# Attention with a soft mixture of experts: which side of the products with v is stationary

## The chip, the cores and the metric

The kernel runs on one core of a Trainium2 chip. The metric is the device time in microseconds (us) of one execution. A core has a matrix engine (TensorE, PE in the profile, its loads of the stationary side PEld), a vector engine (DVE), a scalar engine (ACT), GpSimd (POOL) and a queue engine (SP) that issues the DMAs. A product takes a stationary side, loaded first, and streams a moving side past it; the result's partitions are the stationary side's columns.

## The reference

```python
def _attn_ref(q, k, v, s):                       # 8 batches, 8 heads, 576 rows, 64 columns
    scores = scale * np.matmul(q, k.transpose(0, 1, 3, 2))
    cum = np.cumsum(np.maximum(s, 0.0), axis=-1)
    bias = -(cum[:, :, :, None] - cum[:, :, None, :])
    scores = np.where(causal, -1000000000.0, scores + np.minimum(bias, 0.0))
    attn = np.exp(scores - np.max(scores, axis=-1, keepdims=True))
    attn = attn / (np.sum(attn, axis=-1, keepdims=True) + 1e-09)
    return np.matmul(attn, v)

def _moe_ref(x, phi, w1, w2):                    # x: 4608 x 512, the heads beside each other
    logits = x @ phi                             # 32 slots, 4 for each of 8 experts
    d = softmax of logits over the rows; c = softmax of logits over the slots
    slot_out[e] = relu((d.T @ x)[e] @ w1[e]) @ w2[e]
    return c @ slot_out
```

(The two softmax lines are shortened to words.) q and k come eight times larger than drawn. All inputs are float32.

## The kernel before, in words

Two heads make a pair: 32 pairs, four to a batch. A pair's head 0 lies on partitions 0 to 63 and head 1 on 64 to 127. The 576 rows are cut into chunks: as keys j = 0 to 4 (four of 128, one of 64).

`scores(p)` (L254 to L434) makes a pair's exponentials. q and k are loaded (`load`, L265), copied in a shorter float32 form (`cast`, L278, ACT) and the rest kept beside it (`low`, L283, DVE). The row maxima come from a first product of q and k (`mx`, L311, PE) reduced on DVE (`red`, L323); `f0`, `f1`, `f2`, `md` (L335 to L361) split the maxima in a high and a low part, turn them, and write them by DMA as extra rows of a small tile `gt`, which also holds two rows of the cumulated s. The scores proper (`s`, L377, 48 products a pair) sum three products of q and k parts and a fourth with `gt`, which adds the bias and subtracts the maximum. ACT takes the exponential out of PSUM (`ex`, L388) and POOL zeroes the masked triangle (`cut`, L395). The exponentials lie in the arena as keys on partitions and queries along the row. POOL then sums them over the key chunks (`z`, L421 to L427), ACT copying the first chunk (L414).

`pair(p)` (L440) makes the output of the attention. v is stationary with its 64 columns of a head, the exponentials of key chunk j move, up to 512 queries at a time: `a` (L478) into y, and `ax` (L467) for the first 64 queries into x. The result has the head's columns on partitions and queries along the row. ACT copies it (L486, L490). `sm` (L507) sums z over the keys with a stationary side that holds one column of ones, for the four pairs of a batch into one bank. Per batch `e1` (L595, L596) adds 1e-9 and takes reciprocals, `rw` (L600) writes them to DRAM, and `rd` (L517) reads them back broadcast to 64 partitions each. `nr` (L540, DVE) scales the result in u; for the last pair `rb` (L528) spreads the reciprocals by products. `nat` (L548) transposes u back to rows on partitions, and `natd` (L555, ACT) copies it into x of the batch.

`batch(b)` (L589) makes logits from u (`lt`, L619, L623), and the softmaxes and the sums over rows (`c0` to `t8`); `t7` (L771) multiplies by x. After all pairs, sit (L941) and the experts' two layers (L954, L988) and the output (L1020 and the copies after it) follow. The experts' weights are 64 tiles of 512 KB: NPRE = 21 are fetched during attention into `pre`; the others go where attention's buffers become free (`room`), the last ones where first-layer weights have been used.

The order of every engine is fixed before the run by `schedule` (L34): each step has an engine, an estimated time, a priority (a table `PR` of offsets on top of 2 x pair), what it must follow, and how many of the six PSUM banks it takes. The y and sum banks are kept apart. `busy` (L914) puts filler products on PE where the plan leaves it idle before the first product with v and after the last.

Of the kernel before, what the change touches and what calls it, by code (L numbers as in the profile page):

```python
# [17 lines left out]
NEG = -3.0e38  # L18
NG = 3

PR = dict(load=-9.063, load_v=-9.132, cast=(9.576, 4.001), cum=-25.895, low=(4.9, 44.265), mx=(-6.08, 10.156, 8.807,
          8.159), red=(2.144, 3.397, 3.057, -37.226), f0=-0.714, f1=30.964, f2=0.529, md=-6.393, s=(-65.95, -10.099,
          -16.585, -0.002), ex=(6.942, -14.568, 1.896, 3.855), cut=(1.377, -17.534, 2.864, 12.095), zc=3.583,
          z=(1.07, -54.955, 7.483, 3.74), ax=102.687, a=(136.656, 0.022, -2.121, 0.386, -0.338), evx=-22.47,
          ev=-3.276, sm=14.037, e1=-1.61, rw=24.679, rd=-39.652, nstep=4.53, nr=1.749, nat=48.432, natd=-28.53,
          lt=-51.395, nat0=116.745, natd0=17.779, c0=4.561, c1=-16.819, soft=15.188, tok=30.263, LA=161.4, ct=1.864,
          T2=-19.79, LP=176.8, gap=0.81401)
NBUF = (2, 2, 2, 1, 5, 2, 3)
NBANK = 6
GAP = 300  # L30
NPRE = 21
# [71 lines left out]
def tile_attn_softmoe(ctx: ExitStack, tc, qk, v, s, phi, w1, w2, cst, out):  # L103
# [37 lines left out]
    NR, NPB, NV, NZ, NU, NQ, NW = NBUF  # L141
    PAD = 64
    size = dict(raw=2 * S, p=3200, u=S, v=640, z=2 * S, r=S, x=NCH * DM)
    place = [(kind, (NP + i) % n) for kind, n in (("raw", NR), ("p", NPB), ("z", NZ), ("v", NV), ("r", NQ), ("u", NU), ("x", 1))
# [10 lines left out]
    def slot(kind, shape, dtype, name):  # L155
        return keep.tile(shape, dtype, tag=kind, name=name, bufs=dict(g=NG, w=NW)[kind])
# [16 lines left out]
    s_sb = reg("x", 0)[0:NH, 0:S]  # L173
    ones_s = reg("x", 0)[0:NH, S:2 * S]
    cum = reg("x", 0)[0:NH, 2 * S:3 * S]
    nc.sync.dma_start(out=s_sb, in_=s)
    nc.vector.memset(ones_s, 1.0)
    nc.vector.tensor_scalar(s_sb, s_sb, 0.0, 8.0, op0=ALU.max, op1=ALU.mult)
    nc.vector.tensor_tensor_scan(out=cum, data0=ones_s, data1=s_sb, initial=0.0,
                                 op0=ALU.mult, op1=ALU.add)  # L180
    cumhl = reg("x", 0)[0:NH, 0:2 * S].rearrange("p (l x) -> p l x", l=2)
    nc.vector.tensor_copy(cumhl[:, 0, :].bitcast(F32R), cum)
    nc.vector.tensor_tensor(cumhl[:, 1, :].bitcast(F32R), cum, cumhl[:, 0, :], op=ALU.subtract)
    cumd = pd.tile([NH, 2, S], F32, tag="cum", name="cumd", bufs=1)


    SQ = S // 8
    onesl = one.tile([128, 4 * HP, 32], F32, name="onesl")
    nc.vector.memset(onesl, 0.0)
    for a in range(4 * HP):  # L190
        nc.vector.memset(onesl[:, a, a:a + 1], 1.0)

    dn = one.tile([128, 2, 128], F32, name="dn")
    nc.vector.memset(dn[64:128, 1, :], 0.0)
    nc.gpsimd.memset(reg("x", 0)[64:128, 0:DM], 0.0)
    for i in range(NV):
        nc.gpsimd.memset(reg("v", i)[64:128, 512:640], 0.0)
    for i in range(NPB):
        nc.gpsimd.memset(reg("p", i).rearrange("p (a x) -> p a x", a=2)[64:128, :, 1536:1600], 0.0)
    ph = one.tile([128, HP, 4 * NS], F32, name="ph")  # L200
# [4 lines left out]
    gs = []  # L205
    for i in range(NG):
        t = slot("g", [128, PAD + 2 * S], F32R, f"g{i}")
        if i == 1:

            mask = one.tile([128, S], F32, name="mask")  # L210
            nc.gpsimd.memset(mask, 0.0)
            nc.gpsimd.affine_select(mask[:, S - 128:S], mask[:, S - 128:S], pattern=[[-1, 128]], compare_op=ALU.is_ge,
                                    fill=NEG, base=0, channel_multiplier=1)
        (nc.vector if i else nc.gpsimd).memset(t.bitcast(F32), 0.0)
        for a in (0, 64):
            nc.gpsimd.memset(t[a:a + 4, 0:KO].bitcast(F32), 1.0)
            nc.gpsimd.memset(t[a:a + 4, KO:].bitcast(F32), -1.0)  # L217
        gs.append(t)
# [5 lines left out]
    ones2 = one.tile([128, 128], F32R, name="ones2")  # L224
    nc.vector.memset(ones2.bitcast(F32), 0.0)
    for a in (0, 64):
        nc.vector.memset(ones2[a:a + 2].bitcast(F32), 1.0)  # L227
    mx = []
    for i in range(3):
        t = one.tile([128, 2, NCH], F32, name=f"mx{i}")  # L230
        nc.vector.memset(t, 0.0)
        mx.append(t)

# [20 lines left out]
    def scores(p):  # L254

        t0 = 2.0 * p
        gt, w = gs[p % NG], ws[p % NW]
# [13 lines left out]
        op(("load", p), "SP", 400, (t0, "load"), load,  # L271
# [8 lines left out]
        def low(i):  # L280
            use("raw", p, NR)
            use("w", p, NW)
            nc.vector.tensor_tensor(w[:, QO + S * (2 + i):QO + S * (3 + i)], st["raw", p][:, i, :],  # L283
                                    w[:, QO + S * i:QO + S * (i + 1)].bitcast(F32), op=ALU.subtract)
        g = old(NW)
        war = [("s", g, i) for i in range(4)] if g is not None else []
        for i in range(2):
            op(("cast", p, i), "ACT", 565, (t0, ("cast", i)), (cast, i), [("load", p)] + war)
            op(("low", p, i), "DVE", 950, (t0, ("low", i)), (low, i), [("cast", p, i)])
# [90 lines left out]
        def ex(i, a):  # L380
            if ("p", p) not in st:
                own("p", p, NPB)
                st["p", p] = reg("p", p % NPB).rearrange("p (a x) -> p a x", a=2)
# [729 lines left out]
```

## Time and profile before

| | us |
|---|---|
| median of 3 runs (440.46 to 441.74) | 441.44 |
| the profiled execution | 441.82 |
| its span, first to last instruction | 440.1 |
| PE busy | 406.3 |
| PE's loads (PEld) busy | 302.5 |
| DVE busy | 309.6 |
| POOL busy | 281.4 |
| ACT busy | 245.4 |

The mean granted clock of TensorE is 0.978. A group of instructions is shown as: line, engine, operation, what is written from what (partitions of the moving side * columns of the stationary side for PE), shape, count | busy time in us, mean time of one in ns | idle time before and what ended it. The time of one product includes its way through the array, so neighbours overlap; their pace is the distance of their starts. In the chain of waits a line is start, length and what ran, in us, and in the timeline start, length from the first start to the last end, and the instructions merged.

### The profile page before, as it was taken

Reading aid. Unit: us, or ns where it says so; the run is one execution under the profiler, and the core shown is the slowest. Engines: PE = TensorE matmul, PEld = TensorE weight load, DVE = VectorE, ACT = ScalarE, POOL = GpSimd, SP = SyncE. Lnnn points to the kernel's source line nnn. Section 1 sums busy time; section 2 is a strip of 40 time slices with the busy share of each in tenths; the row PEclk is TensorE's granted clock in tenths of the full one; section 3 lists DMA queues with packets and bytes.
Section 4 is the critical chain, followed back from the end, with each engine's and each line's share of the span. In section 5 each row is a group of like instructions: output and inputs, shape, how many; then the busy total and the mean of one; then the engine's idle time right before and its main releaser. Section 6 shows DMA issues by size and latency. Waiting matters only on the chain.

```text
span 440.1 us, 14686 instructions
## 1 busy us (share of the span) xinstructions
PE 406.3 (92%) x5625; PEld 302.5 (69%) x5625; DVE 309.6 (70%) x1055; ACT 245.4 (56%) x732; POOL 281.4 (64%) x385
## 2 busy tenths in 40 slices
PE   7999999989999999999999999999999999898960
PEld 6787777777677767766877687777776857344550
DVE  6777767987887888779877887788778486121460
ACT  3146676576658665856675676567665745011350
POOL 7349889878877895888588858887887710000000
PEclk9599999999999999999999999999999999999995
DMA  5317565626664475448544822362247389999988
GB/s 175 108 57 236 157 174 155 212 87 189 193 180 131 137 217 157 131 136 225 152 132 136 231 90 84 105 178 82 87 114 216 95 291 337 392 402 409 384 297 293
DMA packets 54549, 83.21 MB, mean 189 GB/s; under 512 B 5456, under 2 KB 41808, under 8 KB 54480
## 3 DMA queue, kind: packets, MB, share of 16 engines
q1 hardware_dynamic: 54480, 82.29, 59.6%
q8 instruction: 44, 0.72, 0.7%
q14 instruction: 25, 0.20, 0.1%
HBM read 71.84 MB, written 10.06 MB: 186 GB/s over the span
## 4 chain that ended last, share of the span: by engine, by line
PE 66%; DMA 12%; DVE 9%; issue 5%; SPq 3%; POOL 2%; ACT 1%; DVEq 0%
PE s L377 19%; PE y L478 15%; PE mx L311 10%; DMA arena<-rs 7%; PE m L954 3%; DMA rs<-sr 3%; PE m L988 3%; PE sum L507 3%; SPq L517 2%; DVE nmin L733 2%; PE busy L914 2%; PE lt L619 2%; PE nat L548 2%; PE po L1020 2%; DVE junk L323 1%
## 5 line engine op out<-in xcount | busy, mean ns | idle before, releaser
L323 DVE CUSTOM_DVE_ANT_0 junk<-mx,mask 128x448 bf16<-128x448 f32 (+3 forms) x320 | 125.5, 427 | 50.8 <-PE mx L311 25.1
L388 ACT ACTIVATE arena<-s 128x288 f32<-128x288 f32 (+4 forms) x384 | 114.3, 409 | 30.0 <-PE s L377 29.3
L377 PE MATMUL s<-w 64*128 64x288 f32 (+4 forms) x1152 | 109.2, 304 | 0.0
L478 PE MATMUL y<-arena 128*64 128x512 f32 (+4 forms) x640 | 90.1, 427 | 0.0
L377 PEld LDWEIGHTS s<-w 64*128 64x128 f32 (+1 forms) x1152 | 81.7, 177 | 10.1 <-ACT arena L388 1.2
L395 POOL TENSOR_SCALAR_AFFINE_SELECT arena<-arena 128x256 f32<-128x256 f32 (+1 forms) x160 | 69.0, 444 | 23.7 <-ACT arena L388 21.7
L478 PEld LDWEIGHTS y<-arena 128*64 128x64 f32 x640 | 43.0, 137 | 46.4 <-issue 35.8
L421 POOL TENSOR_TENSOR arena<-arena 128x896 f32<-128x896 f32 x31 | 66.4, 2141 | 7.5 <-PE mt L346 5.2
L311 PE MATMUL mx<-w 64*128 64x288 f32 (+4 forms) x384 | 59.3, 314 | 3.7 <-DVE e_nat L664 2.7
L311 PE MATMUL mx<-g,ones 64*128 64x288 f32 (+4 forms) x384 | 56.0, 308 | 1.7 <-DVE ones L227 1.7
L377 PE MATMUL s<-g 64*128 64x288 f32 (+4 forms) x384 | 56.5, 291 | 0.0
L423 POOL TENSOR_TENSOR arena<-arena 128x640 f32<-128x640 f32 x31 | 48.0, 1547 | 2.6
L278 ACT CAST w<-arena 128x576 fp32r<-128x576 f32 x64 | 39.8, 675 | 15.0 <-DMA arena<-in_qk_dram 15.0
L283 DVE TENSOR_TENSOR w<-arena,w 128x576 fp32r<-128x576 f32 x64 | 48.0, 776 | 0.0
L311 PEld LDWEIGHTS mx<-w 64*128 64x128 f32 x384 | 41.1, 190 | 8.1 <-PE s L377 3.8
L490 ACT COPY arena<-y 128x512 f32<-128x512 f32 x32 | 18.8, 588 | 47.0 <-PE y L478 47.0
L311 PEld LDWEIGHTS mx<-g,ones 64*128 64x128 f32 x384 | 41.0, 191 | 2.4 <-POOL g L217 1.9
L540 DVE TENSOR_TENSOR arena<-arena 128x576 f32<-128x576 f32 x31 | 34.7, 1128 | 8.7 <-DMA arena<-rs 8.4
L377 PEld LDWEIGHTS s<-g 64*128 64x128 f32 (+1 forms) x384 | 35.1, 177 | 0.7 <-DMA g<-hl 0.2
L338 POOL TENSOR_SCALAR mh<-mx 128x10 fp32r<-128x10 f32 x32 | 21.5, 672 | 20.4 <-DVE mx L323 20.3
L425 POOL TENSOR_TENSOR arena<-arena 128x384 f32<-128x384 f32 x31 | 31.4, 1013 | 2.4
L323 DVE CUSTOM_DVE_ANT_0 junk<-mx,mask,mx 128x288 bf16<-128x288 f32 x64 | 30.6, 516 | 2.2 <-PE mx L311 1.2
(157 smaller groups left out, 565.8 us busy)
## 6 DMA issues: line engine op xcount, KB each, us to landing
pre<-in_w_dram SPq DMA_DIRECT2D x38, 512.0 KB
arena<-in_qk_dram SPq DMA_DIRECT2D x32, 576.0 KB
arena<-in_w_dram SPq DMA_DIRECT2D x18, 512.0 KB
arena<-rs SPq DMA_DIRECT2D x62, 144.0 KB
arena<-in_v_dram SPq DMA_DIRECT2D x32, 256.0 KB
out_dram<-arena SPq DMA_DIRECT2D x11, 512.0 KB
out_dram<-pre SPq DMA_DIRECT2D x7, 512.0 KB
wg<-in_w_dram SPq DMA_DIRECT2D x5, 512.0 KB
```

The source lines that it names most:

```text
L278: nc.scalar.copy(w[:, QO + S * i:QO + S * (i + 1)], st["raw", p][:, i, :])
L283: nc.vector.tensor_tensor(w[:, QO + S * (2 + i):QO + S * (3 + i)], st["raw", p][:, i, :], w[:, QO + S * i:QO + S * (i + 1)].bitcast(F32), ...
L311: nc.tensor.matmul(ps[a][:, d:d + hi - lo], l[r], t[r, KO + lo:KO + hi], start=t is w, stop=t is gt)
L323: nc.vector.tensor_tensor_reduce(out=junk[r, 0:w], in0=ps[r, d:d + w], in1=mask[r, o:o + w], scale=1.0, scalar=m[:, a, 4:5] if i == 1 else ...
L377: nc.tensor.matmul(ps[a][0:n, d:d + hi - lo], t[r, ko + 128 * j:ko + 128 * j + n], t[r, qo + lo:qo + hi], start=x == 0, stop=x == 3)
L388: nc.scalar.activation(st["p", p][0:n, a, o + lo:o + hi], ps[0:n, d:d + hi - lo], AF.Exp, bias=0.0, scale=0.125)
L395: nc.gpsimd.affine_select(d, d, pattern=[[0, 2], [1, n]], compare_op=ALU.is_ge, fill=0.0, base=0, channel_multiplier=-1)
L421: eng.tensor_tensor(z[:, :, 128:576], pt[:, :, 128:576], pt[:, :, 576:1024], op=ALU.add)
L423: eng.tensor_tensor(z[:, :, 256:576], z[:, :, 256:576], pt[:, :, 1024:1344], op=ALU.add)
L425: eng.tensor_tensor(z[:, :, 384:576], z[:, :, 384:576], pt[:, :, 1344:1536], op=ALU.add)
L478: nc.tensor.matmul(y[r, lo - 64:512], vt[:, j, r], st["p", p][:, g, OFF[j] + lo - 128 * j:OFF[j] + 576 - 128 * j], start=(j == 0), stop=(j ...
L540: nc.vector.tensor_tensor(u, u, st.pop(("r", p)), op=ALU.mult)
```

## The change

The exponentials become the stationary side, 128 queries at a time, and v moves: the 64 columns of a head and a 65th column of ones beside them. The result has queries on partitions, in two banks: y0 for the query chunks 0 to 2 and y1 for 3 and 4, both heads side by side. Query chunk c needs the key chunks 0 to c. The 65th column is the row sum, so `z`, `sm`, `e1`, `rw`, `rd`, `rb` and `nr` go, with their buffers; `norm` on DVE adds 1e-9, takes the reciprocal and multiplies out of PSUM. `nat` now turns rows on partitions into columns on partitions for `lt`, which follows it. The query chunks are 0 to 3 of 128 rows and 4 of 64.

`gt`, the ones beside it, the mask and the split maxima become bfloat16; the cumulated s takes three rows instead of two. One of a pair's two `low` steps goes from DVE to POOL. v comes in three DMAs instead of two. NPRE goes from 21 to 26, with smaller buffers in the arena and the `gt` tiles no longer used for weights. Pair 0 gets precedence over all else in the plan, the setup is reordered, and the plan's priorities are another set.

```diff
-NBUF = (2, 2, 2, 1, 5, 2, 3)
+NBUF = (2, 2, 2, 5, 6, 3)
-NPRE = 21
+NPRE = 26
...
-    size = dict(raw=2 * S, p=3200, u=S, v=640, z=2 * S, r=S, x=NCH * DM)
+    size = dict(raw=2 * S, p=3264, u=512, v=650, x=NCH * 128)
...
+    cumhl = scr[:, 0:3 * S // 2].bitcast(BF16).rearrange("p (l x) -> p l x", l=3)
+    for l in range(3):
+        nc.vector.tensor_copy(cumhl[:, l, :], cum)
+        if l < 2:
+            nc.vector.tensor_tensor(cum, cum, cumhl[:, l, :], op=ALU.subtract)
...
-        t = slot("g", [128, PAD + 2 * S], F32R, f"g{i}")
+    gs = [one.tile([128, PAD + 2 * S], BF16, name=f"g{i}") for i in range(NG)]
...
+        nc.gpsimd.memset(x[:, :, :, 64:65], 1.0)
...
+        tu = t0 - 200 * (p == 0)
...
-            nc.vector.tensor_tensor(w[:, QO + S * (2 + i):QO + S * (3 + i)], st["raw", p][:, i, :],
+            (nc.vector if i else nc.gpsimd).tensor_tensor(w[:, QO + S * (2 + i):QO + S * (3 + i)], st["raw", p][:, i, :],
                                     w[:, QO + S * i:QO + S * (i + 1)].bitcast(F32), op=ALU.subtract)
...
-            nc.tensor.transpose(ps[0:4 * NCH, 0:128], mh.rearrange("p a l c -> p (a l c)").bitcast(F32), ident)
+            st["mt", p] = ps[0:4 * NCH, 0:64].bitcast(BF16)
+            nc.tensor.transpose(st["mt", p], mh.rearrange("p a l c -> p (a l c)"), identb)
...
+    yb = [psy.tile([128, 512], F32, tag=f"y{i}", name=f"y{i}") for i in range(2)]
...
+            for g in range(2):
+                c = 128 * hp + 64 * g
+                nc.sync.dma_start(out=vt[:, 0:4, g, 0:64],
+                                  in_=v[b * S:b * S + 512, c:c + 64].rearrange("(j p) c -> p j c", p=128))
+            nc.sync.dma_start(out=vt[0:64, 4, :, 0:64],
+                              in_=v[b * S + 512:b * S + 576, 128 * hp:128 * hp + 128].rearrange("p (g c) -> p g c", g=2))
...
-            for g in range(2):
-                r = slice(64 * g, 64 * g + 64)
-                nc.tensor.matmul(y[r, lo - 64:512], vt[:, j, r],
-                                 st["p", p][:, g, OFF[j] + lo - 128 * j:OFF[j] + 576 - 128 * j],
-                                 start=(j == 0), stop=(j == 4))
+        def av(c):
+            vt = st["v", p]
+            x = reg("p", p % NPB)
+            for g in range(2):
+                y = yb[c // 3][:, 130 * (c % 3) + 65 * g:130 * (c % 3) + 65 * g + 65]
+                for j in range(c + 1):
+                    o = 1600 * g + OFF[j] + 128 * (c - j)
+                    nc.tensor.matmul(y, x[:, o:o + 128], vt[:, j, g, :], start=(j == 0), stop=(j == c))
+
+        def norm(i):
+            n = 3 - i
+            y = yb[i][:, 0:130 * n].rearrange("p (c g d) -> p c g d", c=n, g=2)
+            r = p2.tile([128, n, 2, 1], F32, tag=f"rc{i}", name=f"rc{i}_{p}")
+            nc.vector.tensor_scalar(r, y[:, :, :, 64:65], 1e-9, None, op0=ALU.add)
+            nc.vector.reciprocal(r, r)
+            nc.vector.tensor_tensor(st["x", p][:, 3 * i:3 * i + n, :].rearrange("p c (g d) -> p c g d", g=2), y[:, :, :, 0:64],
+                                    r.broadcast_to([128, n, 2, 64]), op=ALU.mult)
...
-        at_ = (860, 752, 540, 325, 112)
+        for c in range(5):
+            op(("a", p, c), "PE", 236 * (c + 1), (t0, ("a", c)), (av, c), need[c] + ([("a", p, c - 1)] if c else []))
+        for i in range(2):
+            op(("n", p, i), "DVE", (680, 540)[i], (t0, ("n", i)), (norm, i),
+               [("a", p, 2 + 2 * i)] + war + ([("cw",)] if 2 <= p < NX else []))
+        op(("nat", p), "PE", 434, (t0, "nat"), nat, [("n", p, 0), ("n", p, 1)], bank=1)
...
+                st["u0", b] = p2.tile([128, HP, 64], F32, tag="u0", name=f"u0{b}", bufs=1)
...
-                nc.tensor.matmul(ps[32 * g:32 * g + 32, :], dn[:, 0, 32 * g:32 * g + 32], xn[:, g + 1, :],
-                                 start=True, stop=False)
+                r = slice(128 * hp, 128 * hp + 128)
+                for g in range(4):
+                    nc.tensor.matmul(ps[32 * g:32 * g + 32, r], dn[:, 0, 32 * g:32 * g + 32], xn[:, g, :],
+                                     start=hp == 0, stop=False, skip_group_check=True)
```

More of the change, by code (lines that the diff above doesn't have):

```diff
@@ L155, in slot @@
     def slot(kind, shape, dtype, name):
-        return keep.tile(shape, dtype, tag=kind, name=name, bufs=dict(g=NG, w=NW)[kind])
+        return keep.tile(shape, dtype, tag=kind, name=name, bufs=NW)
     def reg(kind, i):
@@ L180, in tile_attn_softmoe @@
                                  op0=ALU.mult, op1=ALU.add)
[L181 to L191, printed above, removed]
@@ L287, in scores @@
         for i in range(2):
[L288 to L289 removed]
+            op(("cast", p, i), "ACT", 565, (tu, ("cast", i)), (cast, i), [("load", p)] + war)
+            op(("low", p, i), "DVE" if i else "POOL", 950 if i else 1400, (t0, ("low", i)), (low, i), [("cast", p, i)])
         def cum():
             for a in range(2):
[L293 removed]
+                nc.sync.dma_start(out=gt[64 * a:64 * a + 3, KO:KO + S],
                                   in_=(cumhl if p < HP else cumd)[2 * p + a:2 * p + a + 1, :, :])
@@ L483, in evx, with nat, natd @@
+        def nat():
+            use("x", p, NX)
+            x = st["x", p]
+            ps = bank(f"nat{p}")
+            st["nat", p] = ps
+            for c in range(4):
+                nc.tensor.transpose(ps[:, 128 * c:128 * c + 128], x[:, c, :], ident)
+        def natd():
             own("u", p, NU)
@@ L589, in batch, with dep_n @@
+        wu = [("lt", p - NU)] if p >= NU else []
+        op(("natd", p), "ACT", 480, (t0, "natd"), natd, [("nat", p)] + wu, frees=[(("nat", p), 0)])
+    def dep_n(p, i):
+        return ("n", p, i) if p >= 0 else None
     def batch(b):
@@ L836, in fetch @@
         nc.sync.dma_start(out=dst, in_=src)
-    for e, ns in (("DVE", 5200), ("POOL", 4200), ("SP", 1100), ("ACT", 2900), ("PE", 1100)):
+    for e, ns in (("DVE", 7000), ("POOL", 6200), ("SP", 700), ("ACT", 2900), ("PE", 1100)):
         op(("set", e), e, ns, (-1000,), lambda: None)
+    for i in range(1, NG):
+        op(("gi", i), "POOL", 2400, (2.0 * i - 10,), (ginit, i), [("set", "POOL")])
     for p in range(NP):
@@ L911, in busy @@
     def busy(n):
-        d = psy.tile([128, 512], F32, tag="y", name="busy")
+        d = yb[0]
         for i in range(n):
@@ L919, in tile_attn_softmoe @@
         if ops[key]["eng"] == "PE":
-            early = early and key[0] not in ("ax", "a")
+            early = early and key[0] != "a"
             n = int((t - end - 200) / GAP)
```

347 lines of the change are left out of this document (100 added, 247 removed).

## The prediction

> **What bounds the kernel now.** I read the page first, then the engines' busy time by stretch, then the products of one source line alone, to count head pairs.
>
> ```profile
> span 440.1 us, 14686 instructions
> ...
> PE 406.3 (92%) x5625; PEld 302.5 (69%) x5625; DVE 309.6 (70%) x1055; ACT 245.4 (56%) x732; POOL 281.4 (64%) x385
> ```
> ```profile
> 11.00:22.00 11.00, 10.04 (x53) 8.22 (x54) 7.92 (x40) 1.44 (x3) 3.82 (x11) 0.53 0.36 108
> 60.00:300.00 240.00, 231.85 (x3464) 177.88 (x3464) 195.18 (x675) 157.11 (x480) 196.46 (x256) 1.00 0.54 155
> 345.00:378.00 33.00, 30.56 (x407) 22.00 (x405) 22.06 (x60) 17.60 (x59) 8.12 (x11) 1.00 0.80 274
> 378.00:420.00 42.00, 39.15 (x442) 19.07 (x442) 10.05 (x17) 7.96 (x15) 0.00 (x0) 1.00 1.03 393
> ```
> ```profile
> 60.00:300.00 240.00, 85.73 (x1096) 71.61 (x1096) 1.00 0.54 155
> ```
>
> The columns of a stretch are its length, then PE, PEld, DVE, ACT and POOL busy time, the granted clock, the DMA share and GB/s. Between 60 and 300 us, the steady part of attention, PE is busy 231.85 of 240 us at clock 1.00; the next engine, POOL, has 196 and DMA 0.54. The last fence is the same stretch for L377 alone: a pair has 48 score products, so 1096 of them are 22.8 pairs, 10.5 us each. PE sets the pace: what the change adds to PE per pair counts 32 times, and what it takes from POOL, DVE, ACT or the queues counts only where PE waits, which is 8.15 us in those 240.
>
> **The products with v, taken out.** The timeline gives the block of L478 from its start to the next block's start; the chain of waits gives L467 and L507.
>
> ```profile
> 207.11 0.66 PE L548 MATMUL nat<-ident,arena 128*128 128x128 f32 x4 [1.05 <-DVE mx L323]
> 207.70 2.81 PE L478 MATMUL y<-arena 128*64 128x512 f32 x20
> 210.44 0.67 PE L377 MATMUL s<-w 64*128 64x288 f32 x6
> ```
> ```profile
> 308.55 0.23 PE x L467 x8
> ...
> 192.55 0.64 PE sum L507 x32
> ```
>
> Ten products of v are 20 instructions, two passes for each float32 product, and take 210.44 − 207.70 = 2.74 us. The x products of two pairs are 0.23, so 0.12 a pair; the row sums are 0.64. Out go 2.74 + 0.12 + 0.64 = 3.50 us of PE per pair.
>
> **The products put in.** Per pair there are 15 blocks (c, j), two heads each, two passes each: 60 instructions. Each now moves only 65 columns, but has 128 columns of exponentials as its own stationary side, where v had 64. What one costs depends on which is longer, the load or the moving side. The trace has no product of just this form, so I bound it from both sides.
>
> ```profile
> L478 PEld LDWEIGHTS y<-arena 128*64 128x64 f32 x640 | 43.0, 137 | 46.4 <-issue 35.8 <-POOL arena L421 1.1 <-POOL arena L395 0.5
> ...
> L548 PEld LDWEIGHTS nat<-ident,arena 128*128 128x128 f32 x128 | 14.2, 141 | 7.4 <-DVE mx L323 6.6 <-PE nat L548 0.5
> ...
> L941 PEld LDWEIGHTS sit<-i4s,acc 128*128 128x128 f32 x8 | 1.0, 191 | 0.9 <-issue 0.9
> ```
> ```profile
> 375.64 0.30 PEld L824 LDWEIGHTS pt<-tot,cst_sb 128*128 128x128 f32 x2 [0.87 <-PE cta L709]
> 376.88 0.97 PEld L941 LDWEIGHTS sit<-i4s,acc 128*128 128x128 f32 x8 [0.94 <-issue]
> ```
>
> By the moving side: v's block moves 1,536 columns in each of two passes in 2.74 us, 0.89 ns a column, so 65 columns take 0.058 us and 60 of them 3.48. By the load: L941 is a float32 product with a full 128*128 stationary side and only 32 moving columns. Its eight loads, 0.191 us each, span 0.97, so they start (0.97 − 0.19) / 7 = 0.111 us apart. L824, with a single moving column, has its two loads (0.30 − 0.19) = 0.11 apart. With 1 or 32 columns the step is the same, so it is the load's, and 65 columns fit inside it. 60 x 0.111 = 6.66 us. I take the load, because L941 is the nearest row: same type, same stationary shape, a short moving side. The net is 6.66 − 3.50 = +3.16 us a pair, +101 us over 32 pairs. Nothing covers it: the load, not an engine beside PE, is the pace.
>
> The Trainium skill, TensorEngine Tiling, section Performance Considerations, advises for a right side of at most 64 columns to swap it to the stationary side and tile by columns. That is the old arrangement, and the change undoes it. The page gives no figure that would move the sum; 64-column loads of 137 ns against full ones of 191 agree with it.
>
> **Boundaries.** The four transposes ahead of y take 0.59 us to y's start; next to other full-array work they take 0.44:
>
> ```profile
> 369.56 0.44 PE nat L548 x4
> ```
>
> A turn into column halves thus costs about 0.15. The new products share the full array with the transposes, but come as five pieces that may be placed apart. Bounds 0 to 0.4 us a pair; I take 0.1, near the end at which they stay together, +3 us.
>
> **PE's old waits.** The 8.15 us in 240 make 10.6 us over 312 us of steady work. With PE slower, DVE and POOL arrive earlier relative to it. I let more than half go, −6; bounds 0 and −10.6.
>
> **DVE, ACT, POOL, queues.** Off them come POOL's sums (L421 and its like), the scaling L540, the copies L414, L486, L490 and the reciprocals' round trip through DRAM. On them go one "low" per pair moved from DVE to POOL, and two norms on DVE.
>
> ```profile
> L421 POOL TENSOR_TENSOR arena<-arena 128x896 f32<-128x896 f32 x31 | 66.4, 2141 | 7.5 <-PE mt L346 5.2
> ...
> L283 DVE TENSOR_TENSOR w<-arena,w 128x576 fp32r<-128x576 f32 x64 | 48.0, 776 | 0.0
> ...
> L540 DVE TENSOR_TENSOR arena<-arena 128x576 f32<-128x576 f32 x31 | 34.7, 1128 | 8.7 <-DMA arena<-rs 8.4
> ```
> ```profile
> L595 DVE TENSOR_SCALAR sr<-sum 128x72 f32<-128x72 f32 x10 | 2.3, 231 | 4.9 <-PE sum L507 3.7 <-DMA rs<-sr 0.7
> ...
> L676 DVE RECIPROCAL cs<-cs 128x5 f32<-128x5 f32 x8 | 1.5, 191 | 0.3
> ...
> L537 DVE TENSOR_TENSOR arena<-arena,rb 128x288 f32<-128x288 f32 x2 | 0.8, 448 | 0.0
> ```
>
> A norm is an add (0.23), a reciprocal (0.19) and a product out of PSUM, 384 or 256 columns; by L537 (288 columns, 0.448) about 0.55 and 0.42. Two norms are 1.8 us, against 0.78 + 1.13 = 1.9 removed, so DVE stays near 195 / 22.8 = 8.6 us a pair, under PE's 10.5 and far under the new 13.7. POOL trades over 2.1 us for about 2141 x 576 / 896 = 1.4. All this is free, hidden by PE. A norm waits on DVE for PE's chunks, and the max reductions queue behind it, with the mx banks behind those; DVE's slack of about 5 us a pair covers that, and without it the wait costs up to a norm, 1 us a pair. The y banks are single, so the next pair's first chunk waits for a norm; nearly a whole pair lies between. The third DMA of v, of 0.6 us like the others on SP, goes where two reads of reciprocals leave.
>
> **Small rows in bfloat16.** The scores keep their column counts. Only narrow products are paced by a load:
>
> ```profile
> 339.87 0.27 PE L377 MATMUL s<-g 64*128 64x192 f32 x2
> 339.98 0.79 PE L377 MATMUL s<-w 64*128 64x448 f32 x6
> 340.61 0.37 PE L377 MATMUL s<-g 64*128 64x448 f32 x2
> ```
>
> 448 columns step 0.63 / 3 = 0.21 us; 192 step 0.11 where columns alone give 0.09. Four such products a pair, two of 64 columns (0.03 by columns), could gain at most 0.2 us a pair, −6 us. No row shows two types in one accumulation; a drain there, of a boundary's size once a pair, would be +5. I take 0, since wide products dominate.
>
> **Start, drain, tail.** The chain near the start holds fillers on PE until the first scores:
>
> ```profile
> 15.69 1.58 PE busy L914 x6
> ...
> 18.04 2.00 PE busy L914 x8
> ...
> 21.25 1.31 PE busy L914 x8
> ...
> 24.02 2.65 PE busy L914 x22
> 26.67 3.39 PE s L377 x48
> ```
>
> The change puts pair 0 ahead of all others and shortens the setup. It can gain at most the fillers' 7.5 us, and nothing if the loads set it; I take −4. In the drain the round trip goes (rs out, rs in, then L540 before lt):
>
> ```profile
> 354.05 6.96 DMA rs<-sr
> ...
> 361.70 4.36 DMA arena<-rs
> ...
> 366.08 0.77 DVE arena L540
> ```
>
> But PE is busy 30.56 of 33 us there, so at most 2.4 go, and lt now waits for norm, transposes and a copy, about 2 us. I take 0, bounds ±2.4. After 378 us DMA is full (1.03) with PE busy 39.15 of 42: five more tiles fetched early take 5 x 0.524 MB / 393 GB/s = 6.7 us from the queue, of which PE's idle time bounds the gain near 2.9 and the last writes a little more; I take −2, bounds 0 and −5.
>
> **The sum**, against the profiled execution's 441.82 us (0.1% over the median of 441.44): 441.8 + 101 + 3 − 6 − 4 − 2 = 534.
>
> **The rivals.** First, the load is hidden or quick. Transposes load the same 128x128 in 141 ns, 50 under L941's, so a step of 0.061 is conceivable; the moving side's 0.058 would then decide. The net is about 0 a pair and the total 441.8 + 0 + 3 − 6 − 4 − 2 = 433, faster. It decides once a float32 load steps below about 0.06. For it: the transposes' row. Against it: L941 and L824, plain products, at 0.11. Chance 0.06. The Trainium skill, TensorE: Matmul & The Clock Gate, section Weight-path perf modes, allows the fast load only for types other than float32, which speaks against this rival, since the exponentials stay float32; the transposes' 141 ns, also float32, are no proof against it, being another operation.
>
> Second, one of the two passes keeps its load and only the other pays 0.111: a mean of 0.085, 60 x 0.085 = 5.07, +1.57 a pair, +50, total 483. Against it: L478 and L941 have a load for every pass. Chance 0.03. The same page, section Back-to-back issue gap, gives about 81 ns for a sustained stream of loads and 128-column products; by that estimate the total would be 476. L941's 0.111 contradicts it for float32.
>
> Third, long runs of loads leave the array underused and the granted clock drops, as at 11 to 22 us (0.53), where loads step twice as far:
>
> ```profile
> 17.97 1.78 PEld L914 LDWEIGHTS busy<-ident 128*128 128x128 f32 x8 [0.28 <-issue]
> ```
>
> 1.78 / 8 = 0.22. The new products would cost 13.2 us a pair and the total near 740. Against it: the clock is 1.00 from 60 to 300 us, and the scores still lie between. Chance 0.03.
>
> **How the numbers follow.** Forecast 0.87, rivals 0.06, 0.03, 0.03, and 0.01 for about no change. All low ends at once (loads at 0.110, no boundaries, waits −10.6, bfloat16 −6, start −7.5, tail −5, drain −2.4) come to 441.8 + 99 − 31.5 = 509; all high ends (boundaries +13, bfloat16 +5, drain +2.4, nothing gained) to 441.8 + 101 + 20 = 563. With 0.13 already outside, hardly more may be left out: 510 to 558. A measurement of this kernel tells apart about 0.3%. Faster 0.06, same 0.01, slower 0.93.
>
> **What would show it.** In the profile after, the exponentials' PEld loads: 1,920 instructions near 190 ns, stepping 0.11 us, and their block near 6.7 us a pair; PE above 98% busy in the steady part at clock 1.00, POOL far lower, a pair near 13.6 us. A step of 0.06 would make the forecast wrong, as would a pair of about 10 us.

## The result and the profile after

The kernel with the change takes 558.38 us (median of 4 runs, 557.59 to 560.68), the kernel before beside it 441.59 us (440.46 to 443.38): a ratio of 1.265, 95% interval 1.259 to 1.271. The profiled execution took 557.6 us. Ratios, here and below, are of the runs that lie within 1.5% of the fastest one of their kernel.

The page of the profile after, its span and its engines, and the windows of the same profile, the first for all engines and the second for the products with v (L441) alone:

```profile
span 555.9 us, 15189 instructions
...
PE 524.5 (94%) x5931; PEld 450.1 (81%) x5931; DVE 317.3 (57%) x1143; ACT 217.2 (39%) x636; POOL 132.7 (24%) x295
```
```profile
60.00:300.00 240.00, 235.67 (x2741) 210.08 (x2740) 148.61 (x557) 101.47 (x304) 63.63 (x137) 1.00 0.35 100
```
```profile
60.00:300.00 240.00, 119.84 (x1020) 116.82 (x1020) 1.00 0.35 100
```

PE is busy 235.67 of 240 us (98.2%) at clock 1.00, POOL only 63.63 where it had 196.46. In those 240 us lie 1020 products of L441; at 60 a pair that is roughly 17 pairs, 14.1 us each, where 22.8 pairs went through before. Next the groups of instructions and the timeline of the profile after, around one pair's products with v:

```profile
L441 PE MATMUL y<-arena 128*128 128x65 f32 x1920 | 225.3, 275 | 0.0
L441 PEld LDWEIGHTS y<-arena 128*128 128x128 f32 x1920 | 219.8, 192 | 4.1
```
```profile
205.18 5.47 PE L441 MATMUL y<-arena 128*128 128x65 f32 x48
...
168.22 1.08 PE L650 MATMUL sl<-arena,dn 128*32 128x128 f32 x32
...
340.90 1.08 PE L650 MATMUL sl<-arena,dn 128*32 128x128 f32 x32
```

There are 1,920 loads of 192 ns, and 48 products span 5.47 us with a last one of 0.275: (5.47 − 0.275) / 47 = 0.111 us a step, the step that the prediction took from L941. The two lines that write `sl` begin `t7` of two batches that lie three batches, 12 pairs, apart: (340.90 − 168.22) / 12 = 14.39 us a pair. The same in the timeline of the profile before:

```profile
149.81 0.61 PE L771 MATMUL sl<-arena,dn 128*32 128x512 f32 x4
...
279.38 1.04 PE L771 MATMUL sl<-arena,dn 128*32 128x512 f32 x8
```

(279.38 − 149.81) / 12 = 10.80. The difference, 3.59 us, times 32 is 115 us, and the span grew by 555.9 − 440.1 = 115.8: the whole loss lies in the steady part. Outside it little moved: the first product with v starts at 31.81 us (31.00 before), from the last one to sit it is 12.53 us (12.47), from sit to the end 63.07 (63.18).

To share out the 3.59, I add up on PE, over these 12 pairs, the time from each product's start to the next one's, without the time in which nothing ran, by the output that the product writes (us a pair):

| output | before | after |
|---|---|---|
| y, x, sum | 3.46 (y 2.66, x 0.19, sum 0.60) | 6.73 |
| s (scores, 48 products) | 3.44 | 3.61 |
| mx (first products for the row maxima, 24) | 1.97 | 2.28 |
| nat, lt, mt, sl and the rest | 1.54 | 1.51 |
| PE idle | 0.40 | 0.27 |
| pair | 10.80 | 14.39 |

The products with v are +3.27, and scores and first products, which the change was not to slow down, +0.47 between them. What slows them is in the timeline of the profile after, for PE and for its loads, over two of the four groups of first products:

```profile
200.95 0.41 PE L313 MATMUL mx<-w 64*128 64x320 f32 x2
201.21 0.31 PE L313 MATMUL mx<-g,ones 64*128 64x320 bf16 x2
201.25 0.36 PE L313 MATMUL mx<-w 64*128 64x192 f32 x2
201.45 0.26 PE L313 MATMUL mx<-g,ones 64*128 64x192 bf16 x2
201.49 0.44 PE L313 MATMUL mx<-w 64*128 64x448 f32 x1
202.23 0.47 PE L313 MATMUL mx<-w 64*128 64x448 f32 x1 [0.30 <-ACT arena L390]
```
```profile
201.20 0.10 PEld L313 LDWEIGHTS <-ones 64*128 64x128 bf16 x2
201.21 0.20 PEld L313 LDWEIGHTS mx<-w 64*128 64x128 f32 x2
```

Two things are to be seen. The bfloat16 load (201.20) begins only when its own product does (201.21), a quarter of a microsecond after the float32 product ahead of it; and the next float32 load comes with that bfloat16 product and not during the products before it. The float32 product of 192 columns (201.25) thus holds PE 0.20 us until its bfloat16 partner starts (201.45). Second, the two heads of the 448-column group do not start together: the second waits for ACT to empty a PSUM bank, and they run one behind the other.

### The profile page after: what moved, and what is told of

The parts are those of the page before. It is cut to its first block, busy times and chain, and to the rows that moved or that the text cites. A ratio compares the mean times of both kernels' runs of the same rounds, so it can differ in the third digit from the quotient of the medians.

```text
span 555.9 us, 15189 instructions
## 1 busy us (share of the span) xinstructions
PE 524.5 (94%) x5931; PEld 450.1 (81%) x5931; DVE 317.3 (57%) x1143; ACT 217.2 (39%) x636; POOL 132.7 (24%) x295
## 4 chain that ended last, share of the span: by engine, by line
PE 80%; ACT 8%; POOL 5%; DVE 2%; DMA 2%; issue 1%; SPq 0%; DVEq 0%; POOLq 0%
PE y L441 39%; PE s L379 16%; PE mx L313 8%; ACT arena L390 7%; POOL arena L397 3%; PE nat L462 3%; PE m L832 3%; PE m L866 2%; PE sl L650 1%; PE po L898 1%; PE lt L497 1%; PE y L792 1%; DMA out_dram<-arena 1%; DMA arena<-in_qk_dram 1%; DVE junk L325 1%
## 5 line engine op out<-in xcount | busy, mean ns | idle before, releaser
L441 PE MATMUL y<-arena 128*128 128x65 f32 x1920 | 225.3, 275 | 0.0
L441 PEld LDWEIGHTS y<-arena 128*128 128x128 f32 x1920 | 219.8, 192 | 4.1
L325 DVE CUSTOM_DVE_ANT_0 junk<-mx,mask 128x448 bf16<-128x448 f32 (+2 forms) x320 | 137.7, 430 | 61.8 <-PE mx L313 44.5
L313 PE MATMUL mx<-g,ones 64*128 64x288 bf16 (+4 forms) x384 | 62.2, 285 | 1.1 <-DMA g<-arena 1.1
L379 PE MATMUL s<-g 64*128 64x288 bf16 (+4 forms) x384 | 59.0, 287 | 0.0
L285 POOL TENSOR_TENSOR w<-arena,w 128x576 fp32r<-128x576 f32 x32 | 45.3, 1415 | 7.6 <-ACT w L280 4.7
L313 PEld LDWEIGHTS <-ones 64*128 64x128 bf16 x384 | 26.3, 93 | 10.3 <-issue 1.3
L379 PEld LDWEIGHTS <-g 64*128 64x128 bf16 (+1 forms) x384 | 21.7, 95 | 13.5 <-issue 2.6
L453 DVE TENSOR_TENSOR arena<-y,rc 128x256 f32<-128x256 f32 (+1 forms) x64 | 31.4, 491 | 2.3
L325 DVE DVE_READ_ACCUMULATOR2_ANT mx<- 128x1 f32 (+1 forms) x384 | 31.3, 82 | 0.0
```

The lines of the kernel that those rows point to most:

```text
L285: (nc.vector if i else nc.gpsimd).tensor_tensor(w[:, QO + S * (2 + i):QO + S * (3 + i)], st["raw", p][:, i, :], w[:, QO + S * i:QO + S * ( ...
L313: nc.tensor.matmul(ps[a][:, d:d + hi - lo], l[r], t[r, KO + lo:KO + hi], start=t is w, stop=t is gt)
L325: nc.vector.tensor_tensor_reduce(out=junk[r, 0:w], in0=ps[r, d:d + w], in1=mask[r, o:o + w], scale=1.0, scalar=m[:, a, 4:5] if i == 1 else ...
L379: nc.tensor.matmul(ps[a][0:n, d:d + hi - lo], t[r, ko + 128 * j:ko + 128 * j + n], t[r, qo + lo:qo + hi], start=x == 0, stop=x == 3)
L441: nc.tensor.matmul(y, x[:, o:o + 128], vt[:, j, g, :], start=(j == 0), stop=(j == c))
L453: nc.vector.tensor_tensor(st["x", p][:, 3 * i:3 * i + n, :].rearrange("p c (g d) -> p c g d", g=2), y[:, :, :, 0:64], r.broadcast_to([128, ...
```

## The experiments

The ratios are against the kernel before, run beside each (its medians lay between 441.8 and 443.6 us). "Pair", "y", "s" and "mx" are worked out as in the table.

**More moving columns.** The products of query chunk c with v move both heads' columns (130) instead of one head's 65, in 56 of 60 instructions; the second half of the result is overwritten by the next product or not used.

```diff
-                    nc.tensor.matmul(y, x[:, o:o + 128], vt[:, j, g, :], start=(j == 0), stop=(j == c))
+                    n = 65 if j == 4 else 130
+                    q = 650 // NCH * j + 65 * g
+                    nc.tensor.matmul(yb[c // 3][:, 130 * (c % 3) + 65 * g:130 * (c % 3) + 65 * g + n], x[:, o:o + 128],
+                                     reg("v", p % NV)[:, q:q + n], start=(j == 0), stop=(j == c))
```

> Each product with v streams 130 columns instead of 65 (56 of the 60 instructions of a pair); the extra columns fall where a later product or nothing is read, so the result is the same. Theory (the load of 128 stationary columns, 0.112 us, is the pace and the stream hides under it): 130 columns need 0.108 us, still under the load, so the step stays 0.112, the period of a pair stays at 14.4 us and the total at 558, within 1%. Rival (the stream, or load and stream one after the other, is the pace): 56 more times 0.054 us, 3.0 us a pair, about 655 us in all.

One run: 563.38 us. In its timeline the same 48 products stand as

```profile
206.06 5.49 PE L443 MATMUL y<-arena 128*128 128x130 f32 x48
```

5.49 us against 5.47, with twice the columns (y 6.82 us a pair instead of 6.73). The load sets the pace, and the moving side is hidden behind it. The total is 0.9% above the change's, within the expected 1%.

**Column halves.** Each product is cut into two with 64 of the exponentials' columns, which write the two halves of the partitions.

```diff
-                    nc.tensor.matmul(y, x[:, o:o + 128], vt[:, j, g, :], start=(j == 0), stop=(j == c))
+                    for h in range(0, 128, 64):
+                        nc.tensor.matmul(y[h:h + 64], x[:, o + h:o + h + 64], vt[:, j, g, :], start=(j == 0), stop=(j == c))
```

> Each product with v is cut into two with 64 stationary columns, side by side in the two column halves of the array; 120 instructions a pair instead of 60, the same sums. Theory (load is the pace, and it goes by columns, and column halves load beside each other): a couple steps by about 0.056 to 0.06 us, the products take 3.5 us a pair instead of 6.73, the period falls from 14.4 to about 11.2 and the total to about 455 us. Rival (a cost for each instruction, or load and stream one after the other): 120 instructions take as long or longer, 558 us or more.

473.54 us, ratio 1.073 (1.065 to 1.080). The groups and the timeline of this run:

```profile
L442 PEld LDWEIGHTS y<-arena 128*64 128x64 f32 x3840 | 117.7, 138 | 10.9 <-issue 6.8
```
```profile
207.69 3.02 PE L442 MATMUL y<-arena 128*64 128x65 f32 x96
```

96 products in 3.02 us, (3.02 − 0.22) / 47 = 0.060 us for each couple of halves: twice the instructions in little over half the time (y 3.84 us a pair instead of 6.73). A load of 64 columns takes 138 ns and two of them go side by side. The step is then near the 0.058 that the prediction worked out for the moving side. The total missed the expected 455: the pair is 11.70 and not 11.2, since y takes 3.84 us and not 3.5, and nat, lt, mt, sl and the rest take 1.71 where the change has 1.51 (nat alone 0.73 and 0.60).

**Small rows back in the shorter float32 form.** The ones, `gt` and the split maxima as before the change, with two rows of the cumulated s; 24 early tiles, for the room they take.

```diff
-    ones2 = one.tile([128, 128], BF16, name="ones2")
+    ones2 = one.tile([128, 128], F32R, name="ones2")
...
-    gs = [one.tile([128, PAD + 2 * S], BF16, name=f"g{i}") for i in range(NG)]
+    gs = [one.tile([128, PAD + 2 * S], F32R, name=f"g{i}") for i in range(NG)]
...
-            mh = p2.tile([128, 2, 2, NCH], BF16, tag="mh", name=f"mh{p}")
+            mh = p2.tile([128, 2, 2, NCH], F32R, tag="mh", name=f"mh{p}")
```

> The small rows go back to the shorter float32 form (extra rows of the scores, the ones, the split maxima, two rows of the cumulated s instead of three); two weight tiles fewer are fetched early, because the rows take more space; all else as changed. Theory (at each change of type PE no longer loads ahead, and this is what s and mx cost more): s and mx fall from 5.88 to 5.40 us a pair, the period from 14.39 to 13.9, the first score starts some 2 us earlier, total about 540 us (-3.2%). Rival (s and mx cost more because the new plan cuts them into other pieces): s and mx stay at 5.9 us a pair, total within 1% of 558.

553.23 us, ratio 1.254 (1.244 to 1.265), pair 14.20. The timeline of this run, for the groups that were shown above, on PE and then one line of its loads:

```profile
213.65 0.31 PE L309 MATMUL mx<-w 64*128 64x320 f32 x2
213.79 0.31 PE L309 MATMUL mx<-g,ones 64*128 64x320 f32 x2
213.94 0.25 PE L309 MATMUL mx<-w 64*128 64x192 f32 x2
214.03 0.27 PE L309 MATMUL mx<-g,ones 64*128 64x192 f32 x2
214.14 0.39 PE L309 MATMUL mx<-w 64*128 64x448 f32 x2
```
```profile
213.65 0.18 PEld L309 LDWEIGHTS mx<-g,ones 64*128 64x128 f32 x2
```

The load of the ones now begins 0.14 us before its product (213.65 and 213.79), and the 192-column product gives way after 0.09 us instead of 0.20. s falls by 0.13, mx by 0.11, and mt (the turn of the maxima, in float32 again) rises by 0.09. So the type explains the scores' loss (0.13 of 0.17) and a third of the first products' (0.11 of 0.31). s and mx together fall from 5.88 to 5.64 and not to 5.40, so the theory had half of it, and the total stays within 1% of 558, as the rival had it. The other 0.2 of mx stays, and with it the wait inside the group. The groups by shape, of this run and then of the kernel before:

```profile
L309 PE MATMUL mx<-w 64*128 64x448 f32 x64 | 23.3, 422 | 7.1 <-ACT arena L386 7.1
```
```profile
L311 PE MATMUL mx<-w 64*128 64x448 f32 x64 | 14.4, 401 | 0.0
```

7.1 us of waiting for ACT where there was none, and 23.3 us busy instead of 14.4, or 0.28 us a pair: this part is not the type. The one-pass run below shows more of it.

**Fewer early tiles.** NPRE is 21, as before the change.

> Only the number of weight tiles fetched early goes back from 26 to 21. Theory (the last stage is paced by PE, not by the weights): the time from the sums of the slots to the end stays at 63 us, total 558 within 0.5%. Rival (the five tiles save queue time that was needed): 3 to 7 us slower.

562.25 us, ratio 1.273 (1.264 to 1.282); from sit to the end 66.0 us instead of 63.1. Taken alone, this would be 3 us for five tiles. But the run with 130 moving columns, which kept all 26, has 66.4 us there, and the other runs of the changed kernel with 24 or 26 tiles have 63.7 to 65.2. The tail differs by that much between runs, so the worth of the tiles stays open.

**One pass.** The exponentials and v in the shorter float32 form of the scores' operands; POOL rounds v once a pair.

```diff
-            vt = st["v", p]
+            vt = vf[p % NV].rearrange("p (j g c) -> p j g c", j=NCH, g=2)
...
+                nc.gpsimd.tensor_scalar(vf[p % NV], reg("v", p % NV), 1.0, None, op0=ALU.mult)
```

(`vf` and the exponentials' buffers, which `reg` now returns, are tiles of that form.)

> The change with the exponentials and v in the shorter float32 form that the scores' q and k have, so that a product with v is one pass instead of two: 30 loads of 128x128 a pair instead of 60 (66 moving columns instead of 65, v rounded by POOL once a pair, 24 early tiles; the output is less exact). Theory, the load is the pace and counts once a pass: 30 x 0.112 = 3.36 us a pair instead of 6.73, period near 11.0, total 558 - 32 x 3.37 = 450 us. Rival, the shorter form loads at the speed of its moving side or not slower than the products of q and k step: 30 x 0.058 = 1.75, total near 399. Second rival, a single pass costs as much as the two did: no change, 558.

472.39 us, ratio 1.069 (1.065 to 1.073), where 450 was expected. The timeline and the windows of this run:

```profile
200.46 2.85 PE L447 MATMUL y<-vf,p 128*128 128x66 f32 x24
```
```profile
108.00:116.00 8.00, 8.00 (x92) 6.89 (x91) 6.35 (x26) 5.55 (x16) 5.51 (x9) 1.00 0.56 169
116.00:124.00 8.00, 8.00 (x62) 6.45 (x61) 4.55 (x20) 2.52 (x10) 3.32 (x6) 0.57 0.62 177
124.00:132.00 8.00, 8.00 (x92) 7.23 (x90) 6.38 (x26) 3.87 (x12) 2.70 (x5) 1.00 0.39 105
132.00:140.00 8.00, 8.00 (x139) 6.99 (x135) 5.33 (x21) 6.20 (x22) 5.05 (x7) 1.00 0.26 79
140.00:148.00 8.00, 8.00 (x89) 6.79 (x88) 4.74 (x19) 1.74 (x6) 1.24 (x5) 0.57 0.59 176
```

At full clock a step is (2.85 − 0.285) / 23 = 0.111 us, and there are half as many: the load costs what it did and counts once a pass. But the granted clock is 0.57 in two of these five windows, 24 us apart, with PE busy in all of them; its mean over the run is 0.888 against 0.989. That is more than the 22 us by which the expectation was missed: if all the time went by the clock, full clock throughout would give 472.4 x 0.888 = 419. Why the clock falls is open.

This run also bears on the 0.2 of mx that the types left. The groups by shape, of the change and then of this run:

```profile
L390 ACT ACTIVATE arena<-s 128x448 f32<-128x448 f32 x64 | 35.0, 546 | 24.0 <-POOL arena L397 24.0
L313 PE MATMUL mx<-w 64*128 64x448 f32 x64 | 24.9, 453 | 8.3 <-ACT arena L390 8.3
```
```profile
L394 ACT ACTIVATE p<-s 128x448 fp32r<-128x448 f32 x64 | 34.3, 543 | 8.3 <-PE s L383 7.5 <-POOL p L403 0.6
L317 PE MATMUL mx<-w 64*128 64x448 f32 x64 | 16.1, 448 | 0.1
```

In the change ACT waits 24.0 us for POOL's `cut` before these exponentials, and PE then 8.3 us for the bank that they free. Here both waits are all but gone, the group takes 16.1 us instead of 24.9, and mx falls from 2.28 to 1.97 us a pair, with the small rows still in bfloat16 and the products on PE in nearly the same order. So what splits the group is that late bank, and the order of PE alone does not bring it about. Which of this run's edits removes ACT's wait is not shown.

**One pass and the small rows in float32.** Both edits, 22 early tiles.

> As the run with one pass, and the small rows (ones, the rows of cumulated s and the split maxima) back in the shorter float32 form (22 early tiles, for lack of room). Theory, the two edits are independent: the small rows were worth 5 us in the two-pass kernel (553.2 against 558.4), so 5 below the one-pass kernel, near 445 us, less 1 or 2 us for the two early tiles given up. Rival, with half the products the pair is no longer bound by PE alone (DVE has about 8.9 us of work a pair) and the order of the plan decides: no difference to the one-pass kernel within 2 us.

Its four runs took 454.7, 461.2, 467.8 and 470.0 us at granted clocks of 0.921, 0.905, 0.890 and 0.886; the ratio, 1.035 (1.025 to 1.045), is of the first two. Time by clock is nearly the same for both, 454.67 x 0.921 = 419 and 461.21 x 0.905 = 417, and 419 in the run before. If all the time went by the clock, the edit would have moved the clock and hardly the work; no run shows that it does. So neither expectation is decided.

**bfloat16 exponentials and v.** The edits of the one-pass run with BF16 for the shorter float32 form; the exponentials stay in the arena.

> The change with the exponentials and v in bfloat16: one pass, 30 loads a pair; the exponentials are rounded to bfloat16, which the output shows. The bfloat16 loads of the small rows take 92 ns where float32 ones take 183 to 198. Theory, the load is the pace by its bytes: a step of 0.112 / 2 = 0.056, about that of 66 moving columns (0.058), 30 x 0.058 = 1.75 us a pair, period near 9.4 if DVE (8.9 us a pair) keeps up, total 558 - 32 x 5 = 400 to 425 us. Rival, bfloat16 loads are not started beside the product before, as with the small rows: 30 x (0.093 + 0.03) = 3.7 us a pair, total near 460. Second rival, a load takes by its columns and not by its bytes: 3.36 us a pair, 450.

427.86 us, ratio 0.967 (0.964 to 0.971): faster than the kernel before. The groups and windows of this run:

```profile
L444 PEld LDWEIGHTS <-arena 128*128 128x128 bf16 x960 | 36.3, 97 | 6.9 <-POOL arena L400 2.2 <-issue 0.3
```
```profile
60.00:300.00 240.00, 210.06 (x3176) 164.67 (x3175) 197.24 (x778) 145.46 (x434) 129.09 (x216) 1.00 0.46 132
```

A load of the same 128x128 takes 97 ns instead of 192, and y 1.09 us a pair: 1.09 / 30 = 0.036 a step, a third of the float32 one for each pass. Here PE is no longer full (210 of 240), and what it waits for most stands in the waits of this run (us, times, longest):

```profile
PE s L380 <- DVE mx L326: 26.9, 51, 0.8
```

That is a bank that DVE has yet to reduce. PE idles 1.32 us a pair instead of the change's 0.27, and the scores take 4.13 instead of 3.61, for a reason that no run isolates; so the pair stays at 10.30 where 9.4 was expected. The Trainium skill, TensorE: Matmul & The Clock Gate, section Weight-path perf modes, has a fast weight load that is on for 128 columns of any type but float32. This run agrees, 97 ns against 192, and the one-pass run shows that the shorter float32 form has no part in it (0.111 a step).

**Another duration in the plan.** The planner's time for a query chunk's products, 0.236 us for each key chunk, becomes 0.4; the chip takes 0.449.

```diff
-            op(("a", p, c), "PE", 236 * (c + 1), (t0, ("a", c)), (av, c), need[c] + ([("a", p, c - 1)] if c else []))
+            op(("a", p, c), "PE", 400 * (c + 1), (t0, ("a", c)), (av, c), need[c] + ([("a", p, c - 1)] if c else []))
```

> The change with one number of its plan altered: the plan took 0.236 us for each key chunk of a product block, the chip takes 0.449; here the plan takes 0.4, so the order of all engines is another one, the work is the same. Open from the run with the small rows in float32: 0.2 us a pair in the first products of q and k that the type does not explain. Theory, the plan's too short blocks put these products where they wait for a bank or split their pairs of heads: period falls from 14.39 by about 0.2 to 14.2, total 552. Rival, the five blocks of y among the scores split them under any order: period 14.4, total 558 within 0.5%.

654.5 us, ratio 1.482 (1.474 to 1.490). The windows of this run:

```profile
120.00:300.00 180.00, 158.36 (x1655) 134.79 (x1658) 92.71 (x361) 57.90 (x177) 38.54 (x79) 0.89 0.27 80
```

PE idles 22 of 180 us, at a clock of 0.89. Both expectations failed: with a duration nearer to the truth the plan became far worse. A likely reason, not shown, is that the priorities belong to the durations they were found with. That the order can cost much is shown. It does not tell what holds the last 0.2 of mx in the change; that rests on the waits shown with the one-pass run.

**The start.** The first two pairs' v is loaded after the second pair's q and k, and both `low` steps of these pairs run on DVE; once with the bfloat16 rows, once with the rows in float32.

```diff
-            (nc.vector if i else nc.gpsimd).tensor_tensor(w[:, QO + S * (2 + i):QO + S * (3 + i)], st["raw", p][:, i, :],
+            (nc.vector if i or p < 2 else nc.gpsimd).tensor_tensor(w[:, QO + S * (2 + i):QO + S * (3 + i)], st["raw", p][:, i, :],
...
-        op(("load_v", p), "SP", 1600, (t0, "load_v"), load_v, war, dma=1000)
+        op(("load_v", p), "SP", 1600, (t0, "load_v"), load_v, war + ([("load", 1)] if p < 2 else []), dma=1000)
```

> The change with two edits of its start: the first two pairs' v is loaded after the second pair's q and k, and both low steps of these two pairs run on DVE. Open is why the start did not become shorter: first score 26.95 us after the change's start, 26.60 before. Theory, v ahead of the second load (which lands at 11.6 us) and POOL's low step beside DVE's (1.55 us instead of 0.75) hold it: first score near 24 us, first y near 29, total 555. Rival, the three-row split of the cumulated s on DVE (to 10.1 us) and the reductions behind it decide: first score stays within 0.5 us of 26.95, total 558.

> The same two edits of the start, with the small rows in the shorter float32 form (two rows of cumulated s, 24 early tiles). The small rows alone gave a first score at 26.43 us and 553.2 us. Theory of the start, the two causes add: first score near 23 us, total 550. Rival, the reductions of the row maxima on DVE, eight a pair, set the first scores whatever comes ahead: first score within 1 us of 26.4, total 553.

558.58 us, ratio 1.257 (1.251 to 1.264), and 550.95 us, ratio 1.243 (1.238 to 1.249). First the timeline of DVE at the start of the change, then of the first of these runs:

```profile
7.50 1.84 DVE L197 TENSOR_TENSOR arena<-arena 64x576 f32<-64x576 f32 x1
9.38 0.75 DVE L195 CAST arena<-arena 64x576 bf16<-64x576 f32 x1
10.05 0.73 DVE L285 TENSOR_TENSOR w<-arena,w 128x576 fp32r<-128x576 f32 x1
12.91 1.55 DVE L285 TENSOR_TENSOR w<-arena,w 128x576 fp32r<-128x576 f32 x1 [2.12 <-ACT w L280]
```
```profile
8.94 0.64 DVE L195 CAST arena<-arena 64x576 bf16<-64x576 f32 x1
9.50 2.74 DVE L285 TENSOR_TENSOR w<-arena,w 128x576 fp32r<-128x576 f32 x4
12.17 0.44 DVE L325 CUSTOM_DVE_ANT_0 junk<-mx,mask 128x288 bf16<-128x288 f32 x1
```

The slow `low` (1.55 us) and the wait for the second load go, and the reductions start at 12.17 instead of 14.38 us, but the first score only at 26.02 instead of 26.95. With the rows in float32 as well it starts at 24.23, the first product with v at 29.02 (31.81 in the change, 31.00 before). In the first score both runs lie between their two expectations. The edits of the start alone give 0.93 us there and the rows alone gave 0.52 (26.43), but both together give 2.72, more than the sum of the two; what keeps the rest is not shown. At the first product with v they are worth 2.8 us together. The first run's gain there (30.37) does not show in its total, where the tail took 64.7 us instead of 63.1.

**bfloat16 products and the rows in float32.** Both edits, 22 early tiles.

> The run with bfloat16 exponentials and v (427.9 us; there y takes 1.09 us a pair, PE waits for DVE 1.34 us a pair, and the first products and the scores take 2.11 and 4.11), with the small rows back in the shorter float32 form, 22 early tiles. Theory, loads of float32 beside float32 are pulled ahead, so the scores and the first products lose about 0.3 us a pair on PE, but DVE's row maxima set the pace: the total stays at 428 within 3 us. Rival, PE is still the bound between the waits: 32 x 0.3 = 10 us less, 418.

421.59 us, ratio 0.951 (0.947 to 0.955), between the two expectations. The pair gains only 0.04 us over three batches (10.27): mx falls by 0.15 and PE's idle time by 0.27, but s rises by 0.38 to 4.51. And 2.1 us come from the start (first product with v at 29.33 instead of 31.43). It is the fastest kernel of this study.

**The turn or the type.** The kernel before, with its own products and bfloat16 exponentials and v; ACT rounds v beside the copy of the first key chunk; 20 early tiles.

```diff
-                st["p", p] = reg("p", p % NPB).rearrange("p (a x) -> p a x", a=2)
+                st["p", p] = reg("p", p % NPB).bitcast(BF16)[:, 0:3200].rearrange("p (a x) -> p a x", a=2)
...
+            nc.scalar.copy(vf[p % NV], reg("v", p % NV))
```

> The kernel before, products with v as they were (v stationary, exponentials move), with the exponentials and v in bfloat16 as in the fastest run so far (421.6 us; ACT rounds v once a pair, 20 early tiles). It tells whether that run is faster for the turn or for the type. Theory, the type does it: y and x are one pass instead of two, 2.66 + 0.19 become half, 1.42 us a pair less on PE, total 442 - 45 = 397 us, faster than the turned products, if no other engine takes over. Rival, POOL's sums over the key chunks (POOL is busy 196.46 of 240 us before) and the fixed order hold the pair at about its old period: total 430 or more, and the turned products in bfloat16 stay ahead.

430.92 us, ratio 0.973 (0.965 to 0.980). y and x fall from 2.85 to 0.88 us a pair, but the pair only to 10.35. The windows of this run:

```profile
60.00:300.00 240.00, 216.26 (x3368) 178.98 (x3367) 199.88 (x702) 180.00 (x537) 190.18 (x268) 0.96 0.55 157
```

PE, DVE, ACT and POOL are all busy between 180 and 216 of 240 us. Of the 1.97 us that y and x save, 0.70 go to PE's idle time (1.10 us a pair instead of 0.40), 0.70 to slower scores and first products (3.82 and 2.29), and 0.12 to the rest. The granted clock is 0.96 here, where it was 1.00, so a part of this is the clock's; the parts are not separated. The total and the comparison came out as the rival had it, but for more reasons than POOL's sums. With the same types (rows in float32) the turned products are ahead, 0.951 against 0.973, the intervals apart. Neither kernel had a plan made for these types.

## Why the prediction was right in kind and wrong in size

Slower, by the loads: that was right, and so was the working of the main term. The time was not: 557.6 us in the profiled execution where the sum gave 534, and a median 0.4 us above the range. The high ends that the prediction listed came to 563, and the range stopped short of them at 558. By the steps of the sum, in us:

| step | predicted | measured |
|---|---|---|
| products with v, net | +101 | 32 x 3.27 = +105 |
| boundaries | +3 | nat, lt, mt, sl and the rest: 32 x −0.03 = −1 |
| small rows in bfloat16, with all else on s and mx | 0 (−6 to +5) | 32 x 0.47 = +15 |
| old waits of PE | −6 | 32 x −0.125 = −4 |
| start | −4 | +0.8 |
| drain, tail | 0, −2 | +0.1, −0.1 |
| sum | +92 | +116 |

**The step that failed** is "small rows in bfloat16": "I take 0, since wide products dominate", with +5 as the worst. It counted the columns of the products and one drain a pair. The runs showed two other things, about half of the +15 each. A change of type to bfloat16 stops the load from running ahead, and there are twelve groups of such products a pair, not one; undone, that gave 0.13 in s and 0.11 in mx, 32 x 0.24 = 8 us. And the 448-column group of the first products falls apart, because ACT, held by POOL, frees its bank late; this is most of the other 0.2. It is gone in the one-pass run, but what brings it about in the change stays open. The prediction had a price for the boundaries of y itself and for a wait on DVE's reductions, and none for a bank that ACT frees late beside y.

**The start** went up 0.8 instead of down 4. The prediction put it down to PE's fillers, which are only what PE does while it waits. The run that moved v's loads and the `low` steps and put the small rows back in float32, two instead of three, gave 2.8 us back; so the change made the start longer by these together, in places (DVE's queue at 6 to 14 us, SP's order) of which the prediction said only that the change "shortens the setup", without a price for the third row.

**The tail** gained nothing in this profile, but it differs by 3 us between runs of the changed kernel, so the term of −2 is neither borne out nor refuted. The prediction counted five more early tiles as 6.7 us off the queue and left out that the change also takes places away: by the code the arena falls from 17 tiles of 4 KB a partition to 16 and the three `gt` tiles no longer take weights, so 21 early tiles and 22 places that come free as attention ends became 26 and 18. No run shows what that is worth.

**The products with v** came out 4 us higher, for a step of 0.112 (6.73 / 60) instead of 0.111 and 3.46 instead of 3.50 taken out: the size of a rounding times 32. **The rivals**: neither a hidden load nor a load for one pass only; float32 pays 0.11 a pass, in two passes and in one. The third rival, a falling clock, stayed out of the change (0.989). The clock did fall in the one-pass run, which has half the loads, so the reason that the rival gave, long runs of loads, is not borne out.

## What to carry to other kernels

Before turning a product round, price it as passes times loads by the stationary side's columns and type, against the moving columns; with few moving columns the loads are the whole price, and here a narrower type (0.036 us a step instead of 0.112) or column halves (0.060 a couple) was worth far more than the products saved elsewhere, the narrower type at a loss of exactness. An edit of types on small operands is not free because they are small: count how often the type changes in PE's order. And when a change moves the blocks of a hand-tuned plan, put a price on the waits of their neighbours too: here a bank that another engine frees late cost as much as the types did.

## What the runs showed of the hardware

A bfloat16 load after a float32 product starts with its own product, and a float32 load after a bfloat16 product no earlier than with it (the loads at 201.20 and 201.21 above), though the bfloat16 load itself is half as long, as the groups of the profile after have it:

```profile
L313 PEld LDWEIGHTS mx<-w 64*128 64x128 f32 x384 | 45.8, 195 | 18.2 <-ACT arena L390 14.7 <-DVE mx L325 2.1 <-issue 0.2
L313 PEld LDWEIGHTS <-ones 64*128 64x128 bf16 x384 | 26.3, 93 | 10.3 <-issue 1.3
```

Two 64-column loads run side by side at 0.060 us a couple, where one of 128 columns takes 0.111. And the clock fell in the one-pass run about every 24 us between 69 and 218 us, to 0.57 over 8 us (0.50 from 117 to 123 us), with PE never idle. The Trainium skill, TensorE: Matmul & The Clock Gate, section HAM oscillation, ties such falls to idle gaps of PE over about 3.4 us; in that run there is none, so the measurement speaks against that rule as the only cause. In the run with another plan, where PE does idle, the clock is low in such stretches, but PE's longest wait in the whole run is 3.0 us, so the rule in this form does not cover that run either; the line of that wait (us, times, longest) and the windows:

```profile
PE mt L349 <- POOL mh L341: 4.0, 3, 3.0
```
```profile
136.00:144.00 8.00, 5.57 (x42) 4.12 (x43) 4.85 (x22) 1.43 (x6) 1.66 (x7) 0.50 0.01 1
...
168.00:176.00 8.00, 8.00 (x75) 8.00 (x75) 4.48 (x16) 1.35 (x5) 0.54 (x2) 1.00 0.86 258
...
184.00:192.00 8.00, 5.55 (x25) 3.15 (x25) 6.71 (x31) 0.00 (x0) 0.46 (x2) 0.68 0.01 2
```
